# Weight conversion split between VectorE and GpSimd, or whole on VectorE; a second tile with a plain float32 second product

## The chip, the cores and the metric

The kernel runs on one core of a Trainium2 chip. The metric is the time of one execution on the device, in microseconds (us), lower is better. Three executions of the kernel before took 537.91 to 540.05 us, with a median of 540.05 us. One more was profiled; its time is 538.55 us, and the span from its first to its last instruction is 536.8 us.

Names used below: PE is TensorE (matrix products and transposes), DVE is VectorE, ACT is ScalarE, POOL is GpSimd, SP is the engine whose queue issues the DMAs. Each engine executes its own instructions in the order in which they were written; between engines there are semaphores.

## The reference

Windowed attention (8 batches, 8 heads, 576 positions, head size 64, each query sees itself and the 63 positions before it) is followed by a dense layer with a SoLU activation, a layer norm and a second product:

```python
scores = q @ k.T / sqrt(64);  masked outside 0 <= i - j < 64
attn = softmax(scores);  x = attn @ v            # x: 4608 tokens x 512
h = x @ w_in                                     # 4608 x 1024
solu = h * softmax(h)
ln = (solu - mean) / sqrt(var + 1e-6) * g_ln
out = ln @ w_out                                 # 4608 x 512, float32
```

**The two weights reach the kernel as 64-bit numbers** (`w_in` 512 x 1024, `w_out` 1024 x 512): the views that the kernel gets are double precision, read as pairs of 32-bit integers, and the kernel itself turns them into float32 by operations on the bits.

## The kernel before

**Tiles.** The 4608 tokens are 36 tiles of 128. For each tile t: scores (PE, into `pS`), masked row maxima (DVE, L396), exponentials (ACT, L401), division by the row sums (POOL, L419; on DVE for tile 0), transposes of the eight 128x128 blocks into `PT` (for tiles 0 to 4 by PE into the two-buffer PSUM tile `t` and copied out by ACT and DVE, L461; later by DMA), values (PE into `pX`, L480), the first product `pH` (PE), the SoLU and the norm (`moe_norm`: DVE L538 takes the row maximum, ACT L540 the exponential, DVE L543 the product with `pH`, ACT L549 the squares, a few small operations, POOL L556 a power and L560 the final scaling of `e`), transposes of `e`, the second product `pO` (PE), copy out and store.

**Products.** PE has a plain float32 product (L512 for the first product, L647 for the second) and a split one: both operands are divided into a high part in a reduced format and a low part that holds the rest, and three products are summed (high x high, high x low, low x high; L523 and L659). `PLAIN_IN = 3` tiles take the plain first product, `PLAIN_OUT = 1` tile the plain second one. The split needs the weights' high and low parts, which the function `split` makes once: for `w_in` four blocks of two halves, ACT L325 makes the high half and a subtraction (L327) the low half, on DVE for the half x = 0 and on POOL for x = 1; for `w_out` ACT L331 and DVE L333. Tiles with the plain second product multiply `g_ln` into `yH` on DVE while they copy it out of PSUM (L627); the others take a copy on ACT (L631) and a subtraction on DVE (L633).

**Weight conversion.** `weight_block` converts one of eight blocks of 128 x 2 x 512 numbers (0 to 3 of `w_in`, 4 to 7 of `w_out`), held in the ring `raw` of four buffers: the absolute value of the high word on ACT (L293), a clamp (L299), a mask and shift (L301), the sign joined in (L303), and the top bits of the low word joined in (L309). For `w_out` (`i >= HELPED`), the block is worked in two halves: ACT L296 shifts the low word, POOL does the clamp (L299) and adds the low word (L306), and DVE does L301 and L303.

**What sets the order.** A planner (`Plan`) is given every operation with its engine, an assumed cost and what it reads and writes, in program order. It lets PE and SP keep their program order (with the exception of some loose PE operations of the first tiles), gives every operation a due time that it derives from PE's, and simulates the engines; each engine then gets its operations in the simulated order. So a changed cost, key or call can move any operation on DVE, ACT and POOL. `RINGS` holds the number of buffers of each tile: `t` has 2, `pH`, `pS` and `pO` 1 each.

**Ahead and behind.** In step t of the main loop, scores and softmax are those of tile t + 3, transposes and values those of t + 1, and the second product is that of t - 2. `cross(t + 3)` (ACT copies and SP's DMA transposes that stand in for PE transposes from tile 5 on) is called last in the step. `split` of `w_out` stands ahead of the second product of tile `PLAIN_OUT`.

Of the kernel before, what the change touches and what calls it, by code (L numbers as in the profile page):

```python
# [37 lines left out]
PLAIN_OUT = 1  # L38
# [5 lines left out]
HELPED = 4  # L44
# [121 lines left out]
def tile_window_attention_solu_moe(  # L166
# [94 lines left out]
    def weight_block(i, src):  # L261

        def raw():
            return T("raw", i, [P, 2, 512, 2], I32)
# [4 lines left out]
        def tf():
            return W32(i)

        def lo():
# [4 lines left out]


        helped = i >= HELPED
        parts = (0, 1) if i == 0 or helped else (slice(0, 2),)
        if i:
            plan.dma(P * 8192, lambda: nc.sync.dma_start(
                raw().rearrange("p a n w -> p a (n w)"), src), [], [("raw", i, x) for x in parts])
        for x in parts:
            n = 1024 if x == slice(0, 2) else 512
            R, W = ("raw", i, x), ("w", i, x) if n == 512 else ("w", i)
            B = R + ("low",)
            if i == 0:  # L290
                plan.dma(P * 8 * n, lambda x=x: nc.sync.dma_start(
                    raw()[:, x].rearrange("p n w -> p (n w)"), src[:, x]), [], [R])
            plan.op("ACT", n + 66, lambda x=x: nc.scalar.activation(  # L293
                tf()[:, x], hi()[:, x].bitcast(F32), AF.Abs), [R], [W])
# [3 lines left out]
            plan.op("POOL" if helped else "DVE", n * 3 // 2 if helped else n // 3 * 2 + 18,
                    lambda x=x: (nc.gpsimd if helped else nc.vector).tensor_scalar(  # L299
                        tf()[:, x], tf()[:, x], EXP_HI, EXP_LO, ALU.min, ALU.max), [W], [W])  # L300
            plan.op("DVE", n // 3 * 2 + 18, lambda x=x: nc.vector.tensor_scalar(  # L301
                t()[:, x], t()[:, x], 0x07FFFFFF, 3, ALU.bitwise_and, ALU.logical_shift_left), [W], [W])
            plan.op("DVE", n + 170, lambda x=x: nc.vector.scalar_tensor_tensor(  # L303
                t()[:, x], hi()[:, x], -0x40000000, t()[:, x], ALU.bitwise_and, ALU.bitwise_or), [R, W], [W])
            if helped:
                plan.op("POOL", n * 2, lambda x=x: nc.gpsimd.tensor_tensor(  # L306
                    t()[:, x], t()[:, x], lo()[:, x], op=ALU.add), [B, W], [W])
            else:
                plan.op("DVE", n + 170, lambda x=x: nc.vector.scalar_tensor_tensor(  # L309
                    t()[:, x], lo()[:, x], 29, t()[:, x], ALU.logical_shift_right, ALU.bitwise_or), [R, W], [W])  # L310
# [8 lines left out]
    def split(i):  # L319

        for x in range(2):
            reads = [("w", i), ("w", i, x), ("w", NC + 1 if i < NC else NW - 1)]
            last = reads[:2] + [("H", i, x)], [("w", NW + i, x)]
            if i < NC:
                plan.op("ACT", 600, lambda x=x: nc.scalar.copy(WH(i, x), W32(i)[:, x]), reads, [("H", i, x)])  # L325
                plan.op("POOL" if x else "DVE", 1050 if x else 620, lambda x=x: (
                    nc.gpsimd if x else nc.vector).tensor_sub(  # L327
# [366 lines left out]
    for t in range(NTILE + BEHIND):  # L694
# [8 lines left out]
        if t < BEHIND:  # L703
# [72 lines left out]
```

## Time and profile before

| what | before |
|---|---|
| three runs, us | 540.05, 537.91, 540.05 |
| the profiled execution, us | 538.55 |
| its span, us | 536.8 |
| PE busy, us | 512.3 (95%) |
| DVE busy, us | 419.3 (78%) |
| ACT busy, us | 358.2 (67%) |
| POOL busy, us | 232.6 (43%) |
| mean granted TensorE clock | 0.993 |

Busy time is a sum over stages that differ. A window table of the same execution divides the span: PE is busy 7.26 of the 10 us from 50 to 60, 7.86 of those from 60 to 70, and all of those from 200 to 480. DVE is busy 10.00 us in each of the stretches 50 to 60 and 60 to 70, and 227.08 of the 280 us from 200 to 480. In rows of the timeline the columns are: start in us, duration in us, engine, line, operation, output and inputs with sizes, count; in brackets the idle time of the engine ahead of the row and what ended it. Rows of one engine may overlap by about 0.1 us, so the step from one start to the next, not the duration, is what an instruction costs its engine when it follows another.

### The profile page before, as it was taken

How to read it: one execution, taken by the hardware profiler on the slowest of the kernel's cores; microseconds unless marked ns; L12 is line 12 of the kernel's file. 1: busy time of each engine (PE TensorE's matmuls, PEld its weight loads, DVE VectorE, ACT ScalarE, POOL GpSimd, SP SyncE). 2: the span in 40 equal slices, each digit the busy share in tenths (PEclk: the TensorE clock that was granted, in tenths of full speed). 3: DMA queues.
4: the chain of work that ended last, by engine and by line, in shares of the span. 5: the costliest groups of instructions: out<-in, count | busy, mean ns of one | idle time of the engine just before them, and what ended most of it. 6: DMA issues, size and time to landing. Idle time of an engine off the chain costs nothing.

```text
span 536.8 us, 11697 instructions
## 1 busy us (share of the span) xinstructions
PE 512.3 (95%) x4080; PEld 396.9 (74%) x4080; DVE 419.3 (78%) x1323; ACT 358.2 (67%) x973; POOL 232.6 (43%) x426
## 2 busy tenths in 40 slices
PE   3779699999999999999999999999999999999997
PEld 2345468777878787877777777777777778787785
DVE  4959998788888788888887878888888888887630
ACT  5598667766766666666666766666666766666331
POOL 2149886244444444444444444444444444444220
PEclk9999799999999999999999999999999999999999
DMA  8992014879778878777788877777679877674411
GB/s 321 409 382 95 20 40 128 188 148 187 163 189 187 187 191 180 197 168 189 180 184 186 191 190 183 186 187 186 175 167 195 205 185 187 180 189 89 78 40 39
DMA packets 148506, 93.56 MB, mean 174 GB/s; under 512 B 132960, under 2 KB 132960, under 8 KB 148064
## 3 DMA queue, kind: packets, MB, share of 16 engines
q1 hardware_dynamic: 148448, 92.83, 68.4%
q8 instruction: 32, 0.52, 0.4%
q14 instruction: 26, 0.21, 0.1%
HBM read 50.86 MB, written 9.44 MB: 112 GB/s over the span
## 4 chain that ended last, share of the span: by engine, by line
PE 89%; DVE 5%; ACT 2%; DMA 2%; issue 1%; POOL 0%; POOLq 0%; DVEq 0%; ACTq 0%
PE pO L659 36%; PE pH L523 34%; PE pS L381 7%; PE pX L480 7%; PE pH L512 3%; PE pO L647 1%; PE pX L659 1%; DMA raw<-raw 1%; DVE w L301 1%; DVE sS L396 1%; DMA qk<-qk 1%; PE t L622 1%; DVE w L303 1%; DVE w L327 1%; ACT w L293 0%
## 5 line engine op out<-in xcount | busy, mean ns | idle before, releaser
L556 POOL TENSOR_TENSOR mst<-mst,neghalf 128x1 f32<-128x1 f32 x36 | 20.7, 574 | 238.7 <-DVE mst L554 238.7
L419 POOL TENSOR_SCALAR sS<-sS,rec 128x128 f32<-128x128 f32 x280 | 112.2, 419 | 20.2 <-DVE nmx L396 17.7
L401 ACT ACTIVATE sS<-sS,nmx 128x128 f32<-128x128 f32 x288 | 112.5, 396 | 7.5 <-DVE nmx L396 7.5
L659 PE MATMUL pO<-w_outH,yH 128*128 128x512 f32 x272 | 111.4, 410 | 0.0
L659 PE MATMUL pO<-w,yH 128*128 128x512 f32 x272 | 107.7, 396 | 0.0
L659 PE MATMUL pO<-w_outH,yL 128*128 128x512 f32 x272 | 107.0, 393 | 0.1
L523 PE MATMUL pH<-w_inH,xH 128*128 128x512 f32 x264 | 105.5, 399 | 0.0
L523 PE MATMUL pH<-w,xH 128*128 128x512 f32 x264 | 104.2, 399 | 0.0
L523 PE MATMUL pH<-w_inH,xL 128*128 128x512 f32 x264 | 103.6, 392 | 0.0
L494 ACT CAST xH<-pX 128x512 fp32r<-128x512 f32 x33 | 19.3, 586 | 115.7 <-PE pX L480 115.7
L560 POOL TENSOR_SCALAR e<-e,mst 128x512 f32<-128x512 f32 x72 | 72.5, 1014 | 17.1 <-DVE rec L414 9.5
L433 ACT COPY raw<-sS 128x1024 uint16<-128x1024 uint16 x62 | 62.2, 1049 | 4.7 <-POOL sS L419 4.7
L538 DVE TENSOR_REDUCE mst<-pH 128x1 f32<-128x1024 f32 x36 | 44.0, 1223 | 25.1 <-PE pH L523 24.1
L659 PEld LDWEIGHTS pO<-w_outH,yH 128*128 128x128 f32 x272 | 51.0, 187 | 16.5 <-issue 5.2
L586 DVE COPY raw<-e 128x1024 uint16<-128x1024 uint16 x62 | 45.5, 735 | 21.6 <-POOL e L560 21.6
L659 PEld LDWEIGHTS pO<-w_outH,yL 128*128 128x128 f32 x272 | 51.1, 188 | 13.1 <-DVE yL L633 0.5
L523 PEld LDWEIGHTS pH<-w_inH,xH 128*128 128x128 f32 x264 | 49.5, 187 | 13.3 <-ACT sS L401 0.2
L523 PEld LDWEIGHTS pH<-w_inH,xL 128*128 128x128 f32 x264 | 49.6, 188 | 12.6 <-issue 0.2
L659 PEld LDWEIGHTS pO<-w,yH 128*128 128x128 f32 x272 | 51.1, 188 | 10.5
L523 PEld LDWEIGHTS pH<-w,xH 128*128 128x128 f32 x264 | 49.6, 188 | 11.4
L401 ACT ACTIVATION_READ_ACCUMULATOR sS<-sS,nmx 128x1 f32 x288 | 55.3, 192 | 0.0
L396 DVE CUSTOM_DVE_ANT_0 sS<-pS,maskNone 128x128 f32<-128x128 f32 x224 | 51.4, 282 | 1.4 <-PE pS L381 1.3
(77 smaller groups left out, 804.3 us busy)
## 6 DMA issues: line engine op xcount, KB each, us to landing
qk<-qk SPq DMA_DIRECT2D x36, 640.0 KB, 4.6
v<-vS SPq DMA_DIRECT2D x36, 512.0 KB, 5.2
y<-ot SPq DMA_DIRECT2D x36, 256.0 KB, 2.5
raw<-w_out SPq DMA_DIRECT2D x4, 1024.0 KB, 9.5
raw<-w_in SPq DMA_DIRECT2D x3, 1024.0 KB, 11.8
raw<-raw SPq DMA_TRANSPOSE x124, 3.2
raw<-w_in SPq DMA_DIRECT2D x2, 512.0 KB, 6.6
g_sb<-gT SPq DMA_DIRECT2D x1, 4.0 KB, 14.2
```

Of the source, the lines that this page charges most:

```text
L381: nc.tensor.matmul(PS(t)[half * WIN:(half + 1) * WIN, r, p], q[rs, p, half * WIN:(half + 1) * WIN], keys, start=True, stop=True)
L396: plan.op("DVE", 215, lambda h=h: nc.vector.tensor_tensor_reduce(SS(t)[:, h], PS(t)[:, h % 2, h // 2], mk, scale=-SCALE, scalar=BIG, op0=A ...
L401: plan.op("ACT", 390, lambda h=h: nc.scalar.activation(SS(t)[:, h], SS(t)[:, h], AF.Exp, bias=cols("nmx", h), scale=-1.0, accum_out=cols(" ...
L419: plan.op(engine, cost, lambda h=h: v.tensor_scalar(SS(t)[:, h], SS(t)[:, h], rec()[:, h:h + 1], 0.0, ALU.mult, ALU.add), [R], [("sS", t, h)])
L433: plan.op("ACT", 1050, lambda x=x: nc.scalar.copy(XP(t)[:, x], SS(t)[:, 4 * x:4 * x + 4].bitcast(U16).rearrange("p h (n w) -> p w (h n)", ...
L480: nc.tensor.matmul(PX(t)[r * D:(r + 1) * D, p, ks], V(t, half)[:, h * D:(h + 1) * D], PT(t)[:, h, ks], start=True, stop=True)
L523: plan.op("PE", 233, lambda n=n, c=c, x=x, w=w: nc.tensor.matmul(PH(t)[:, hs], x(t)[:, c], WH(c, h) if w is WH else WL(c)[:, h], start=(n ...
L538: plan.op("DVE", 1150, lambda: nc.vector.tensor_reduce(nmax(), PH(t), axis=AX.X, op=ALU.max, negate=True), [("pH", t)], [key(0)])
L556: plan.op("POOL", 560, lambda: nc.gpsimd.tensor_tensor(kk(), kk(), neghalf, op=ALU.pow), [], [key(5)])
L560: plan.op("POOL", 770, lambda h=h, hs=hs: nc.gpsimd.tensor_scalar(E(t)[:, hs], E(t)[:, hs], nmean(), kk(), ALU.add, ALU.mult), [key(4), ke ...
L586: plan.op("DVE", 740, lambda h=h: nc.vector.tensor_copy(EP(t, h), E(t)[:, h * 512:(h + 1) * 512].bitcast(U16).rearrange("p (n w) -> p w n" ...
L659: plan.op("PE", 233, lambda f=f, i=i, x=x, k=k, y=y, w=w: nc.tensor.matmul(PO(), y(t)[:, f], w(i, x), start=(f == k == 0), stop=(f == NF - ...
```

## The change

- `weight_block` has one form again: all eight blocks are converted on DVE (clamp, mask and shift, sign, low word), blocks 1 to 7 whole (1024 elements a partition), block 0 in its two halves. ACT's shift of the low word (L296) and POOL's clamp (L299) and addition (L306) are gone.
- The low parts of `w_in` (L327 before, L310 after) are all made on DVE.
- `PLAIN_OUT` is 2: tile 1 too takes the plain second product, and `split` of `w_out` moves one step later with it.
- `cross` is called right behind the softmax of its tile, ahead of the second product of that step, where it was called at the end of the step.

```diff
-PLAIN_OUT = 1
+PLAIN_OUT = 2
-HELPED = 4
...
-        helped = i >= HELPED
-        parts = (0, 1) if i == 0 or helped else (slice(0, 2),)
-        if i:
-            plan.dma(P * 8192, lambda: nc.sync.dma_start(
-                raw().rearrange("p a n w -> p a (n w)"), src), [], [("raw", i, x) for x in parts])
+        parts = (0, 1) if i == 0 else (slice(0, 2),)
         for x in parts:
...
             plan.op("ACT", n + 66, lambda x=x: nc.scalar.activation(
                 tf()[:, x], hi()[:, x].bitcast(F32), AF.Abs), [R], [W])
-            if helped:
-                plan.op("ACT", n + 66, lambda x=x: nc.scalar.mul(
-                    lo()[:, x], lo()[:, x].bitcast(U32), 2.0 ** -29), [R], [B])
-            plan.op("POOL" if helped else "DVE", n * 3 // 2 if helped else n // 3 * 2 + 18,
-                    lambda x=x: (nc.gpsimd if helped else nc.vector).tensor_scalar(
-                        tf()[:, x], tf()[:, x], EXP_HI, EXP_LO, ALU.min, ALU.max), [W], [W])
+            plan.op("DVE", n // 3 * 2 + 18, lambda x=x: nc.vector.tensor_scalar(
+                tf()[:, x], tf()[:, x], EXP_LO, EXP_HI, ALU.max, ALU.min), [W], [W])
...
-            if helped:
-                plan.op("POOL", n * 2, lambda x=x: nc.gpsimd.tensor_tensor(
-                    t()[:, x], t()[:, x], lo()[:, x], op=ALU.add), [B, W], [W])
-            else:
-                plan.op("DVE", n + 170, lambda x=x: nc.vector.scalar_tensor_tensor(
-                    t()[:, x], lo()[:, x], 29, t()[:, x], ALU.logical_shift_right, ALU.bitwise_or), [R, W], [W])
+            plan.op("DVE", n + 170, lambda x=x: nc.vector.scalar_tensor_tensor(
+                t()[:, x], lo()[:, x], 29, t()[:, x], ALU.logical_shift_right, ALU.bitwise_or), [R, W], [W])
...
-                plan.op("POOL" if x else "DVE", 1050 if x else 620, lambda x=x: (
-                    nc.gpsimd if x else nc.vector).tensor_sub(
+                plan.op("DVE", 620, lambda x=x: nc.vector.tensor_sub(
                     WL(i)[:, x], W32(i)[:, x], WH(i, x).bitcast(F32)), *last)
...
+    def attend(t):
+        on(scores, t + AHEAD)
+        on(softmax, t + AHEAD)
+        on(cross, t + AHEAD)
...
-            on(scores, t + AHEAD)
-            on(softmax, t + AHEAD)
+            attend(t)
...
-        on(cross, t + AHEAD)
```

In the changed kernel the lines stand 8 to 17 earlier: L299 is L287, L301 L289, L303 L291, L309 L293, L327 L310, L396 L379, L419 L402, L461 L444, L538 L521, L543 L526, L627 L610, L622 L605, L647 L630, L523 L506.

What the planner makes of it is shown at three places. In the names, the first number is that of the tile or block (`w_5` is weight block 5, `w_8` to `w_11` are the low parts of blocks 0 to 3, `PT_3` belongs to token tile 3), the second one is only an identifier.

The first place is DVE ahead of the copy of `PT_3`, the second half of tile 3's transposed weights. Before:

```order
L303 SCALAR_TENSOR_TENSOR w_5_443<-raw_5_310,w_5_443 128x512
L301 TENSOR_SCALAR w_5_443<-w_5_443 128x512
L327 TENSOR_TENSOR w_8_206<-w_0_151,w_inH_103 128x512
L303 SCALAR_TENSOR_TENSOR w_5_443<-raw_5_310,w_5_443 128x512
L301 TENSOR_SCALAR w_6_549<-w_6_549 128x512
L327 TENSOR_TENSOR w_9_596<-w_1_192,w_inH_103 128x512
L303 SCALAR_TENSOR_TENSOR w_6_549<-raw_6_377,w_6_549 128x512
L301 TENSOR_SCALAR w_6_549<-w_6_549 128x512
...
L303 SCALAR_TENSOR_TENSOR w_6_549<-raw_6_377,w_6_549 128x512
...
L301 TENSOR_SCALAR w_7_584<-w_7_584 128x512
L461 COPY PT_3_564<-t_13_616 128x512
```

and after:

```order
L291 SCALAR_TENSOR_TENSOR w_5_432<-raw_5_304,w_5_432 128x1024
L289 TENSOR_SCALAR w_6_448<-w_6_448 128x1024
L293 SCALAR_TENSOR_TENSOR w_5_432<-raw_5_304,w_5_432 128x1024
L291 SCALAR_TENSOR_TENSOR w_6_448<-raw_6_367,w_6_448 128x1024
L287 TENSOR_SCALAR w_7_468<-w_7_468 128x1024
L293 SCALAR_TENSOR_TENSOR w_6_448<-raw_6_367,w_6_448 128x1024
L289 TENSOR_SCALAR w_7_468<-w_7_468 128x1024
L444 COPY PT_3_559<-t_13_588 128x512
```

The rows ahead of the first one are, in both kernels, the eight row maxima of tile 4 with L543 of tile 1 among them. The two subtractions for the low parts of `w_in` no longer stand ahead of the copy, and the conversions are whole blocks.

The second place is the rest of that stretch on DVE, behind the copy, after the change:

```order
L521 TENSOR_REDUCE mst_2_604<-pH_2_557 128x1
L610 TENSOR_TENSOR yH_0_628<-t_2_598,g_sb_105 128x512
L291 SCALAR_TENSOR_TENSOR w_7_468<-raw_7_412,w_7_468 128x1024
L610 TENSOR_TENSOR yH_0_628<-t_3_606,g_sb_105 128x512
L293 SCALAR_TENSOR_TENSOR w_7_468<-raw_7_412,w_7_468 128x1024
L526 ISA e_2_630,mst_2_604<-pH_2_557,e_2_630 128x1024
...
L478 TENSOR_TENSOR xL_3_664<-pX_3_611,xH_3_652 128x512
L310 TENSOR_TENSOR w_8_668<-w_0_151,w_inH_103 128x512 x2
L397 TENSOR_SCALAR rec_4_674<-sm_4_541 128x8
L310 TENSOR_TENSOR w_9_678<-w_1_193,w_inH_103 128x512 x2
L400 RECIPROCAL rec_4_674<-rec_4_674 128x8
L310 TENSOR_TENSOR w_10_685<-w_2_208,w_inH_103 128x512 x2
```

Behind these stand the last two L310 (`w_11`). All eight low parts of `w_in` are now made in one run here, where four of them stood on POOL and two of DVE's four stood ahead of the copy.

The third place is POOL, whose rows between the scaling of tile 3's and tile 4's attention weights were, before:

```order
L419 TENSOR_SCALAR sS_3_407<-sS_3_407,rec_3_496 128x128 x8
L299 TENSOR_SCALAR w_5_443<-w_5_443 128x512
L306 TENSOR_TENSOR w_4_436<-w_4_436,raw_4_275 128x512
L299 TENSOR_SCALAR w_6_549<-w_6_549 128x512
L306 TENSOR_TENSOR w_5_443<-w_5_443,raw_5_310 128x512
...
L306 TENSOR_TENSOR w_7_584<-w_7_584,raw_7_419 128x512
L327 TENSOR_TENSOR w_11_715<-w_3_268,w_inH_103 128x512
L419 TENSOR_SCALAR sS_4_534<-sS_4_534,rec_4_695 128x128 x8
```

and are, after, with the rows around them:

```order
L539 TENSOR_TENSOR mst_0_334<-mst_0_334,neghalf_106 128x1
L543 TENSOR_SCALAR e_0_356<-e_0_356,mst_0_334 128x512 x2
L402 TENSOR_SCALAR sS_3_401<-sS_3_401,rec_3_495 128x128 x8
L402 TENSOR_SCALAR sS_4_518<-sS_4_518,rec_4_674 128x128 x8
L539 TENSOR_TENSOR mst_1_477<-mst_1_477,neghalf_106 128x1
```

Nothing is left between the two L402. PE's rows behind tile 1's second product, 1651 up to the last instruction, read alike in both kernels; the 24 split products of tile 1's second product (L659) are eight plain ones (L630). In the profile a plain product of 512 columns shows as two instructions, so that eight of them count 16.

More of the change, by code (lines that the diff above doesn't have):

```diff
@@ L14 @@
 I32 = mybir.dt.int32
-U32 = mybir.dt.uint32
 AF = mybir.ActivationFunctionType
@@ L278, in hi @@
             return raw()[:, :, :, 1]
-        helped = i >= HELPED
-        parts = (0, 1) if i == 0 or helped else (slice(0, 2),)
-        if i:
-            plan.dma(P * 8192, lambda: nc.sync.dma_start(
-                raw().rearrange("p a n w -> p a (n w)"), src), [], [("raw", i, x) for x in parts])
-        for x in parts:
[L287 to L292, printed above, removed]
+        parts = (0, 1) if i == 0 else (slice(0, 2),)
+        for x in parts:
+            n = 1024 if i else 512
+            R, W = ("raw", i, x), ("w", i) if i else ("w", i, x)
+            plan.dma(P * 8 * n, lambda x=x: nc.sync.dma_start(
+                raw()[:, x].rearrange("p a n w -> p a (n w)" if i else "p n w -> p (n w)"), src[:, x]), [], [R])
             plan.op("ACT", n + 66, lambda x=x: nc.scalar.activation(
                 tf()[:, x], hi()[:, x].bitcast(F32), AF.Abs), [R], [W])
-            if helped:
-                plan.op("ACT", n + 66, lambda x=x: nc.scalar.mul(
-                    lo()[:, x], lo()[:, x].bitcast(U32), 2.0 ** -29), [R], [B])
-            plan.op("POOL" if helped else "DVE", n * 3 // 2 if helped else n // 3 * 2 + 18,
-                    lambda x=x: (nc.gpsimd if helped else nc.vector).tensor_scalar(
-                        tf()[:, x], tf()[:, x], EXP_HI, EXP_LO, ALU.min, ALU.max), [W], [W])
+            plan.op("DVE", n // 3 * 2 + 18, lambda x=x: nc.vector.tensor_scalar(
+                tf()[:, x], tf()[:, x], EXP_LO, EXP_HI, ALU.max, ALU.min), [W], [W])
             plan.op("DVE", n // 3 * 2 + 18, lambda x=x: nc.vector.tensor_scalar(
@@ L718, in tile_window_attention_solu_moe @@
             on(values, t + 1)
-            on(scores, t + AHEAD)
-            on(softmax, t + AHEAD)
+            attend(t)
             if t - BEHIND == PLAIN_OUT:
```

## Prediction

> **What bounds the kernel now.** I read the page's chain of waits first, then windows of PE with the granted clock, then the timelines of PE, DVE and POOL where PE stands still.
>
> ```profile
> span 536.8 us, 11697 instructions
> ...
> PE 89%; DVE 5%; ACT 2%; DMA 2%; issue 1%; POOL 0%; POOLq 0%; DVEq 0%; ACTq 0%
> ...
> 50.00:62.00 12.00, 7.26 (x23) 0.97 0.16 64
> 62.00:68.00 6.00, 5.86 (x69) 0.50 0.25 87
> 68.00:74.00 6.00, 6.00 (x15) 0.98 0.01 1
> ...
> 200.00:480.00 280.00, 280.00 (x2335) 223.53 (x2334) 227.08 (x738) 193.89 (x534) 121.70 (x231) 1.00 0.77 185
> ```
>
> The window columns are stretch, length, PE busy with its count, and, in the first three rows, clock, DMA share and GB/s. The chain is PE for 89%, and PE is busy all of 200 to 480 us, so the steady part is PE's own work. What can be won lies ahead of it: from 50 to 62 PE works 7.26 of 12 us, and then 6 us pass at half clock. The order of events on PE:
>
> ```profile
> 49.28 6.25 PE L512 MATMUL pH<-w,xH 128*128 128x512 f32 x14 [0.34 <-DVE mst L543]
> 55.36 0.60 PE L456 MATMUL t<-ident,sS 128*128 128x128 f32 x4
> ...
> 56.66 0.60 PE L622 MATMUL t<-ident,e 128*128 128x128 f32 x4
> 62.14 1.12 PE L622 MATMUL t<-ident,e 128*128 128x128 f32 x4 [4.88 <-DVE PT L461]
> 63.19 1.98 PE L480 MATMUL pX<-PT,v 128*64 128x64 f32 x32
> 65.10 1.99 PE L381 MATMUL pS<-qk 64*64 64x128 f32 x32
> 67.02 7.70 PE L647 MATMUL pO<-w,yH 128*128 128x512 f32 x16
> 74.15 0.79 PE L523 MATMUL pH<-w_inH,xH 128*128 128x512 f32 x1
> ...
> 81.01 1.03 PE L622 MATMUL t<-ident,e 128*128 128x128 f32 x8
> 81.97 1.15 PE L480 MATMUL pX<-PT,v 128*64 128x64 f32 x32
> 83.05 1.10 PE L381 MATMUL pS<-qk 64*64 64x128 f32 x32
> 84.09 0.50 PE L659 MATMUL pO<-w_outH,yH 128*128 128x512 f32 x1
> ...
> 89.80 0.40 PE L523 MATMUL pH<-w_inH,xH 128*128 128x512 f32 x1
> ```
>
> PE stands 4.88 us until DVE's copy of `PT` (L461) frees a buffer of `t`. The same three groups at 62.14 and at 81.01 show what the low clock costs on top: from start to start 1.05 against 0.48 us for four transposes (half of the 0.96 for eight), 1.91 against 1.08, 1.92 against 1.04.
>
> Why is the copy late?
>
> ```profile
> 45.20 0.77 DVE L414 TENSOR_SCALAR rec<-sm 128x8 f32<-128x8 f32 x1
> ...
> 50.99 1.52 DVE L301 TENSOR_SCALAR w<-w 128x512 int32<-128x512 int32 x1
> 52.44 1.09 DVE L327 TENSOR_TENSOR w<-w,w_inH 128x512 fp32r<-128x512 f32 x1
> 53.45 1.79 DVE L303 SCALAR_TENSOR_TENSOR w<-raw,w 128x512 int32<-128x512 int32 x1
> ...
> 61.41 0.68 DVE L461 COPY PT<-t 128x512 f32<-128x512 f32 x1
> ...
> L303 DVE SCALAR_TENSOR_TENSOR w<-raw,w 128x512 int32<-128x512 int32 x8 | 9.0, 1126 | 0.0
> L538 DVE TENSOR_REDUCE mst<-pH 128x1 f32<-128x1024 f32 x2 | 2.4, 1218 | 0.4 <-PE pH L512 0.4
> L543 DVE CUSTOM_DVE_ANT_0 e<-pH,e 128x1024 f32<-128x1024 f32 x2 | 2.4, 1214 | 0.0
> ...
> 50.49 1.73 POOL L306 TENSOR_TENSOR w<-w,raw 128x512 int32<-128x512 int32 x1
> 52.96 1.73 POOL L306 TENSOR_TENSOR w<-w,raw 128x512 int32<-128x512 int32 x1
> ```
>
> DVE is not idle, but its instructions last far longer than the work in them. L301 starts at 50.99 and ends at 52.51, just behind POOL's L306 (50.49 to 52.22); L303 of 53.45 lasts 1.79, and POOL's next L306 ends at 54.69. The same operations with POOL idle, twice as wide:
>
> ```profile
> 24.73 0.69 DVE L299 TENSOR_SCALAR w<-w 128x1024 f32<-128x1024 f32 x1 [0.41 <-ACT w L293]
> 25.34 0.28 DVE L396 CUSTOM_DVE_ANT_0 sS<-pS,maskNone 128x128 f32<-128x128 f32 x1
> ...
> 25.55 0.69 DVE L301 TENSOR_SCALAR w<-w 128x1024 int32<-128x1024 int32 x1
> ...
> 26.36 1.22 DVE L303 SCALAR_TENSOR_TENSOR w<-raw,w 128x1024 int32<-128x1024 int32 x1
> ...
> 28.31 1.22 DVE L309 SCALAR_TENSOR_TENSOR w<-raw,w 128x1024 int32<-128x1024 int32 x1
> 29.45 0.17 DVE L414 TENSOR_SCALAR rec<-sm 128x8 f32<-128x8 f32 x1
> ```
>
> A whole block costs 1.22 us where a half takes 1.126 us in the mean beside POOL. From start to start, the clean costs are 0.61 (L299, and L301 alike), 0.21 (L396) and 1.14 us (L309, and L303 alike).
>
> The Trainium skill, SBUF — State Buffer, section "SBUF: two separate sides", says that the two engines share a port pair that one instruction holds to its end while the other engine blocks. By that rule the stall above is POOL's doing, and the rows agree; it also speaks against part of the change, below.
>
> **The change part by part.**
>
> *DVE up to the copy.*
>
> ```profile
> 40.66 0.57 DVE L557 TENSOR_TENSOR mst<-mst 128x1 f32<-128x1 f32 x1 [2.79 <-POOL mst L556]
> ```
>
> Up to L414 at 45.20 I move nothing: the first `w_out` block, 2 x 0.61 + 2 x 1.14 = 3.5 us, goes mostly into this idle time of 2.79, and what it pushes back is ahead of L538 of tile 1, which waits for PE. From 45.20 to the copy DVE then has L414, L417 and one L301 (0.9 together), eight L396 (8 x 0.21 = 1.7), L543 (1.15), four block operations of two tensors (4 x 1.14 = 4.6) and three of one (3 x 0.61 = 1.8): 10.2 us, so the copy starts at 55.4 and ends at 56.0, where it was 61.41. POOL has in this stretch only the eight L419 of tile 3; DVE's L396, L414 and L543 stand beside them.
>
> *PE at the stall.* L543 of tile 1, for which PE waited at 49.28, ends some 0.8 us earlier, since DVE's first rows from 45.20 lose the waits for POOL. So all of PE moves by 0.8: the first L622 starts at 55.85 and the second can at 56.3, when the copy is there. PE goes on at 56.3 instead of 62.14: 5.8 us. Nothing is left that would bring the clock down, so the half-clock excess goes too: 0.57 + 0.83 + 0.88, and for L647, 7.13 from start to start against 16 x 0.434 = 6.95 at full clock ((55.36 - 49.28)/14 = 0.434), 0.18 more: 2.5 us. The first product of tile 3, at 74.15 before, would start at 74.15 - 8.3 = 65.8.
>
> *The plain second product.* 16 x 0.434 = 6.95 us replace 24 split products, 89.80 - 84.09 = 5.71: 1.24 us more on PE, uncovered. On DVE L627 takes the place of L633, alike in kind. The low parts of `w_out` are due 14 us later.
>
> *The low parts of `w_in`.* All eight now stand behind L543 of tile 2 and in front of PE's first split product. Behind the copy DVE has L538 (it waits for PE until 56.0), L627 twice, two block operations, L543, L495: I count 56.1 + 1.15 + 2 x 0.6 + 2 x 1.14 + 1.15 + 0.6 = 62.5, then eight L327 at 0.6 and about 0.5 of small ones: the seventh ends at 67.2, the last at 67.8. PE wants the seventh after eight high products and three low ones (11 x 0.238, from 5.71/24): 65.8 + 2.6 = 68.4. But POOL's eight L419 for tile 4 start in the middle of them:
>
> ```profile
> 69.54 0.67 DVE L327 TENSOR_TENSOR w<-w,w_inH 128x512 fp32r<-128x512 f32 x1
> ...
> 37.30 2.80 POOL L419 TENSOR_SCALAR sS<-sS,rec 128x128 f32<-128x128 f32 x8 [4.39 <-DVE nmx L396]
> 72.11 3.67 POOL L419 TENSOR_SCALAR sS<-sS,rec 128x128 f32<-128x128 f32 x8
> ...
> 77.34 3.04 POOL L560 TENSOR_SCALAR e<-e,mst 128x512 f32<-128x512 f32 x2 [0.51 <-DVE mst L557]
> ```
>
> Alone an L419 takes 2.80/8 = 0.35, at 72.11, with DVE at work, 0.46. At best nothing is lost; at worst each of the four or five L327 left waits for one L419, 0.35 each, 1.8 us, and the seventh is 0.6 late. The norm of tile 1 (L552, L556, L560) stands behind this and is wanted at 65.8 + 24 x 0.238 + 0.96 of transposes = 72.5; its two L560 took 3.04 us beside DVE, and I count them ready between 72.3 and 73.9, up to 1.4 late. So 0 to 2.0 us of new idle time; I take 0.7, since most of the excess is measured at 0.11 an L419.
>
> By the skill's rule of the held port, L327 with its two SBUF inputs and L419 exclude each other in full; that is the 2.0 end.
>
> *No cost.* ACT loses eight L296, POOL its clamps, additions and subtractions, neither of which ended the stall. Calling `cross` earlier puts SP's transposes ahead of a store that nothing on the chip waits for; the loads stay behind both. What hides it is PE's work: were SP to hold a load, PE would stop in each of some 30 steps.
>
> *Sum* against the profiled execution, 538.55: -8.3 + 1.24 + 0.7 = -6.4, so 532.2. It lies 1.5 below the median of the three runs, which reach from 537.91 to 540.05; midway between 532.2 and 540.05 - 6.4 = 533.7 I forecast **533.0 us**.
>
> **The rivals.**
>
> 1. *The queue of low parts becomes the wait.* All eight L327 wait for an L419 each (2.8 us): the seventh is 1.3 late, and the norm of tile 1, 2.8 behind and slowed, 2.2 more: idle of 3.5 instead of 0.7, 535.0 on the profile, about 535.8. For it: DVE's longest run of two-input operations now lies right ahead of the first split product. Against: POOL begins only after the fourth L327.
>
> The Trainium skill, TensorE: Matmul & The Clock Gate, section "What's actually happening", has the clock halved after an idle window of about 3.4 us; by it, this rival's 3.5 us in one piece would cost the 2.5 of the low clock as well, 538.3. The 4.88 us above agree with it.
>
> 2. *Slower: DVE's times were no contention.* If the 1.126 of a half block is its price in this stage, work given back to a full engine makes it later. DVE's rows of 45.20 to 61.41 are 9.7 us at the clean costs and took 16.2, a factor of 1.68; with it the copy starts at 45.2 + 17.1 = 62.3, 0.9 later than before; the run from there to the seventh L327, 11.8 us clean, takes 19.8 and ends at 82.1; PE, at low clock, wants it at 63.4 + 4.9 + 7.1 + 2.6 = 78.0, a wait of 4; the plain product adds 1.24: +6, 543 to 546. The case decides where DVE needs over 16.2 us from L414 to the copy. Against it: 1.22 for a whole block with POOL idle.
>
> 3. *Given back later.* The front is 6.4 us earlier, but SP's new order (transposes, then store) makes PE wait in the steady part, by 0.2 us in each of 30 tiles: 538 to 540, no change. Against: PE had no idle time in 280 us, and its order there is the same.
>
> **How the numbers follow.** Forecast 0.64, rival 1 0.20, rival 2 0.07, rival 3 0.09. A measurement of this kernel can tell about 0.5% (2.7 us) from no change, so faster means under 537.3: the forecast and most of rival 1, 0.81; same: rival 3 and the edge of rival 1, 0.12; slower 0.07. The range: no new idle and the lower runs give 531, with 1.5 us for the spread of runs 529.5; above, it takes in rival 1 and the beginning of rival 3: 538.0. All the range but its last 0.7 us lies on the side of faster.
>
> **What would show it.** DVE's `PT` copy at about 55.4, without an idle row of over 1 us in PE ahead of the second L622; clock 1.00 from 56 to 68; L630 as 16 in about 6.95 us from about 59; `pH` of tile 3 at 66, and of tile 4 at 83 to 84 (89.80 before). L291 at 1.22 whole would settle rival 2. Idle time on PE with L310 or L543 as releaser at 67 to 75 would be rival 1; PE idle behind 100 us rival 3. I am wrong if the copy is not before 58 or a gap of over 3 us opens elsewhere.

## Result and the profile after

| | before | after |
|---|---|---|
| runs, us | 537.91 to 540.05, median 539.86 (4 runs) | 530.94 to 533.39, median **531.04** (4 runs) |
| ratio, 95% interval | 1 | **0.9855** [0.982, 0.9891] |
| profiled execution, span, us | 536.8 | 531.6 |
| PE busy; DVE; ACT; POOL, us | 512.3; 419.3; 358.2; 232.6 | 511.5; 415.4; 352.4; 213.9 |

The changed kernel is faster by 1.1 to 1.8%. The forecast was 533.0 us with a range of 529.5 to 538.0. Three executions that took far longer than the others of their kernel (873.66 us of the kernel before, 2703.8 and 572.57 us in two of the experiments) are left out of all medians and ranges here and below. The page of the changed kernel, and its window table of PE (stretch, length, busy time and count of PE, PEld, DVE, ACT, POOL, then clock, DMA share and GB/s):

```profile
span 531.6 us, 11607 instructions
...
PE 94%; ACT 2%; DVE 2%; DMA 1%; POOL 0%; issue 0%; ACTq 0%; DVEq 0%
...
20.00:30.00 10.00, 7.76 (x60) 3.77 (x60) 7.71 (x27) 4.98 (x20) 0.00 (x0) 0.83 1.02 405
50.00:62.00 12.00, 12.00 (x98) 6.95 (x97) 12.00 (x19) 10.27 (x28) 0.68 (x2) 1.00 0.39 139
62.00:68.00 6.00, 6.00 (x16) 2.80 (x16) 6.00 (x15) 3.79 (x7) 1.19 (x2) 1.00 0.02 10
```

PE now works 12.00 of the 12 us from 50 to 62 (7.26 before), and the stretch from 62 to 68 is at clock 1.00 (0.50 before). DVE's share of the chain fell from 5% to 2%. But a stretch from 20 to 30 us is at 0.83, which no stretch of before was at that time. PE's timeline of this execution shows a group of four products that lasts 3.41 us, where the same group took 1.98 before:

```profile
24.91 3.41 PE L495 MATMUL pH<-w,xH 128*128 128x512 f32 x4 [1.00 <-ACT xH L473]
```

The first transfer also landed 0.6 us later in this execution (PE's first product at 5.17 us, 4.54 before). A second profiled execution of the same changed kernel, with a span of 529.3 us and its first product at 4.56, has no such group, so its rows can be laid beside those of before. PE:

```profile
47.74 6.18 PE L495 MATMUL pH<-w,xH 128*128 128x512 f32 x14
...
55.06 1.04 PE L605 MATMUL t<-ident,e 128*128 128x128 f32 x8
56.02 1.15 PE L463 MATMUL pX<-PT,v 128*64 128x64 f32 x32
57.10 1.10 PE L364 MATMUL pS<-qk 64*64 64x128 f32 x32
58.14 7.13 PE L630 MATMUL pO<-w,yH 128*128 128x512 f32 x16
64.71 0.80 PE L506 MATMUL pH<-w_inH,xH 128*128 128x512 f32 x1
...
67.90 1.51 PE L439 MATMUL t<-ident,sS 128*128 128x128 f32 x8
...
72.95 0.65 PE L605 MATMUL t<-ident,e 128*128 128x128 f32 x4 [0.32 <-POOL e L543]
...
75.65 7.13 PE L630 MATMUL pO<-w,yH 128*128 128x512 f32 x16
82.22 0.80 PE L506 MATMUL pH<-w_inH,xH 128*128 128x512 f32 x1
82.86 0.40 PE L506 MATMUL pH<-w,xH 128*128 128x512 f32 x1
```

The wait of 4.88 us is gone: all eight L605 run in one piece. DVE ahead of it:

```profile
44.51 0.16 DVE L397 TENSOR_SCALAR rec<-sm 128x8 f32<-128x8 f32 x1
...
51.10 1.21 DVE L291 SCALAR_TENSOR_TENSOR w<-raw,w 128x1024 int32<-128x1024 int32 x1
52.24 0.68 DVE L287 TENSOR_SCALAR w<-w 128x1024 f32<-128x1024 f32 x1
52.84 1.21 DVE L293 SCALAR_TENSOR_TENSOR w<-raw,w 128x1024 int32<-128x1024 int32 x1
53.97 0.68 DVE L289 TENSOR_SCALAR w<-w 128x1024 int32<-128x1024 int32 x1
54.58 0.68 DVE L444 COPY PT<-t 128x512 f32<-128x512 f32 x1
```

The whole block costs 1.21, and the copy starts at 54.58 (61.41 before), 10.07 us behind L397; 10.2 were forecast.

### The profile page after: what moved, and what is told of

It is laid out like the page before. It is cut to its first block, busy times and chain, and to the rows that moved or that the text cites. A ratio compares the mean times of both kernels' runs of the same rounds, so it can differ in the third digit from the quotient of the medians.

```text
span 531.6 us, 11607 instructions
## 1 busy us (share of the span) xinstructions
PE 511.5 (96%) x4072; PEld 393.2 (74%) x4072; DVE 415.4 (78%) x1327; ACT 352.4 (66%) x959; POOL 213.9 (40%) x406
## 4 chain that ended last, share of the span: by engine, by line
PE 94%; ACT 2%; DVE 2%; DMA 1%; POOL 0%; issue 0%; ACTq 0%; DVEq 0%
PE pO L642 36%; PE pH L506 34%; PE pX L463 7%; PE pS L364 7%; PE pH L495 4%; PE pO L630 3%; PE pX L642 1%; DMA qk<-qk 1%; PE t L605 1%; ACT sS L384 1%; PE t L439 1%; ACT w L285 0%; POOL e L543 0%; DVE mst L521 0%; ACT e L523 0%; ACT PT L444 0%
## 5 line engine op out<-in xcount | busy, mean ns | idle before, releaser
L402 POOL TENSOR_SCALAR sS<-sS,rec 128x128 f32<-128x128 f32 x280 | 116.9, 439 | 49.8 <-DVE nmx L379 27.0
L642 PE MATMUL pO<-w_outH,yH 128*128 128x512 f32 x264 | 108.1, 410 | 0.0
L506 PE MATMUL pH<-w_inH,xH 128*128 128x512 f32 x264 | 105.8, 401 | 0.0
L642 PE MATMUL pO<-w,yH 128*128 128x512 f32 x264 | 104.6, 396 | 0.0
L506 PE MATMUL pH<-w,xH 128*128 128x512 f32 x264 | 104.2, 399 | 0.0
L642 PE MATMUL pO<-w_outH,yL 128*128 128x512 f32 x264 | 103.7, 393 | 0.0
L506 PE MATMUL pH<-w_inH,xL 128*128 128x512 f32 x264 | 103.6, 392 | 0.0
L543 POOL TENSOR_SCALAR e<-e,mst 128x512 f32<-128x512 f32 x72 | 73.5, 1028 | 18.4 <-DVE rec L397 11.0
L521 DVE TENSOR_REDUCE mst<-pH 128x1 f32<-128x1024 f32 x36 | 44.0, 1224 | 26.0 <-PE pH L506 25.2
L569 DVE COPY raw<-e 128x1024 uint16<-128x1024 uint16 x62 | 46.6, 752 | 21.9 <-POOL e L543 21.9
L642 PEld LDWEIGHTS pO<-w_outH,yH 128*128 128x128 f32 x264 | 49.5, 187 | 16.0 <-issue 5.0
L506 PEld LDWEIGHTS pH<-w_inH,xH 128*128 128x128 f32 x264 | 49.5, 188 | 13.5 <-issue 0.5
L506 PEld LDWEIGHTS pH<-w_inH,xL 128*128 128x128 f32 x264 | 49.6, 188 | 12.6 <-DVE w L310 0.2
L642 PEld LDWEIGHTS pO<-w_outH,yL 128*128 128x128 f32 x264 | 49.6, 188 | 12.3
L506 PEld LDWEIGHTS pH<-w,xH 128*128 128x128 f32 x264 | 49.6, 188 | 11.6 <-issue 0.2
L642 PEld LDWEIGHTS pO<-w,yH 128*128 128x128 f32 x264 | 49.6, 188 | 10.2
L379 DVE CUSTOM_DVE_ANT_0 sS<-pS,maskNone 128x128 f32<-128x128 f32 x224 | 51.1, 281 | 4.0 <-PE pS L364 3.9
```

The lines of the kernel that those rows point to most:

```text
L379: plan.op("DVE", 215, lambda h=h: nc.vector.tensor_tensor_reduce(SS(t)[:, h], PS(t)[:, h % 2, h // 2], mk, scale=-SCALE, scalar=BIG, op0=A ...
L402: plan.op(engine, cost, lambda h=h: v.tensor_scalar(SS(t)[:, h], SS(t)[:, h], rec()[:, h:h + 1], 0.0, ALU.mult, ALU.add), [R], [("sS", t, h)])
L506: plan.op("PE", 233, lambda n=n, c=c, x=x, w=w: nc.tensor.matmul(PH(t)[:, hs], x(t)[:, c], WH(c, h) if w is WH else WL(c)[:, h], start=(n ...
L521: plan.op("DVE", 1150, lambda: nc.vector.tensor_reduce(nmax(), PH(t), axis=AX.X, op=ALU.max, negate=True), [("pH", t)], [key(0)])
L543: plan.op("POOL", 770, lambda h=h, hs=hs: nc.gpsimd.tensor_scalar(E(t)[:, hs], E(t)[:, hs], nmean(), kk(), ALU.add, ALU.mult), [key(4), ke ...
L569: plan.op("DVE", 740, lambda h=h: nc.vector.tensor_copy(EP(t, h), E(t)[:, h * 512:(h + 1) * 512].bitcast(U16).rearrange("p (n w) -> p w n" ...
```

## Experiments

The kernel before ran beside each of them, with medians of 538.6 to 538.9 us; a ratio is the time of a run over that of the kernel before, with its 95% interval. Line numbers of a run can stand a few higher than in the kernel it was made from. "Added" instructions work on a spare tile whose contents nothing reads, or on a PSUM buffer that is overwritten later, so that they change no result.

### The parts of the change alone

The conversion alone, in the kernel before:

```diff
-HELPED = 4
+HELPED = 8
```

> The kernel before, with the conversion of w_out whole on DVE (no GpSimd, no ScalarE part in it) and nothing else changed: the low parts of w_in stay divided between DVE and GpSimd, one tile has the plain second product. My theory (the stall before the second L622, and the low clock behind it, come from GpSimd's conversions holding up DVE): the PT copy of tile 3 comes some 5 us earlier, PE does not stand still there, clock 1.00 from 56 to 68, and the time falls by 6.5 to 8.5 us against the kernel before. Rival (the moved low parts of w_in are what freed DVE ahead of the copy): less than half of the gain, 536 to 538. Rival (the plain second product of tile 1 is needed for the gain, since w_out's low parts have to be made in 70 to 80 us): the stall moves to the second product of tile 1, 535 to 538.

Measured: 534.02 us (533.51 to 535.18), ratio 0.9906 [0.9893, 0.9919]. The conversion alone brings two thirds of the gain, less than was expected. PE's timeline tells why:

```profile
57.98 0.66 PE L622 MATMUL t<-ident,e 128*128 128x128 f32 x4 [0.73 <-DVE PT L461]
...
75.99 0.66 PE L622 MATMUL t<-ident,e 128*128 128x128 f32 x4 [0.87 <-POOL e L560]
...
92.23 1.28 PE L480 MATMUL pX<-PT,v 128*64 128x64 f32 x32 [1.15 <-issue]
94.34 1.10 PE L381 MATMUL pS<-qk 64*64 64x128 f32 x32 [0.83 <-DMA qk<-qk]
```

The wait for the copy is 0.73 instead of 4.88, but PE, earlier now, runs into the next waits: POOL's scaling of `e`, and at 92 to 94 tile 5's transposed weights and loads. Even the 0.73 has the old cause: one POOL subtraction (L327, 53.07 to 55.03 us) is left ahead of the copy, and DVE's L299 beside it, at 53.83, takes 1.76 us, where the changed kernel's takes 0.68.

The plain second product alone, in the kernel before:

```diff
-PLAIN_OUT = 1
+PLAIN_OUT = 2
```

> The kernel before, with the plain second product for tile 1 too and nothing else changed. My theory: PE gets 1.24 us more work and the stall at 57 to 62 us stays: 1 to 1.5 us slower than before. Rival (the plain product takes work from DVE and ScalarE at a crowded place and gains by itself): 0.5 to 2 us faster.

Measured: 539.75 us (538.26 to 541.17, 11 runs), ratio 1.0018 [1.0007, 1.0028], 0.4 to 1.5 us slower. PE's wait is 4.88 as before, and 62 to 68 us are at clock 0.50. So alone it costs about what was put down for it, and the rival's gain did not come.

The whole change without the plain second product of tile 1:

```diff
-PLAIN_OUT = 2
+PLAIN_OUT = 1
```

> The changed kernel with the plain second product for tile 0 alone, as before the change. My theory (the second plain product costs PE 1.24 us and buys nothing): 1.0 to 1.3 us faster than the changed kernel, about 529.8. Rival (the eight low parts of w_out, 5.3 us of DVE, then fall due right behind those of w_in, and PE waits for them): as slow as the changed kernel or slower, 531 to 533, with PE idle on L316 at 78 to 83 us.

Measured: 536.71 us (534.66 to 538.82, 12 runs), ratio 0.9958 [0.9944, 0.9973]. It is 5.5 us slower than the changed kernel where 1.0 to 1.3 faster was expected. **The theory of an edit that only costs fell here.** PE has no idle time at the old stall in this run either, nor does it wait for L316 at 78 to 83 us as the rival had it. It loses the time later:

```profile
90.30 1.09 PE L463 MATMUL pX<-PT,v 128*64 128x64 f32 x16 [2.13 <-issue]
92.07 1.12 PE L463 MATMUL pX<-PT,v 128*64 128x64 f32 x16 [0.67 <-DVE PT L426]
93.67 1.99 PE L364 MATMUL pS<-qk 64*64 64x128 f32 x32 [0.48 <-DMA qk<-qk]
```

DVE's and SP's timelines of the same run say what is late:

```profile
78.97 1.40 DVE L316 SCALAR_TENSOR_TENSOR w<-w,g_sb,w_outH 128x512 fp32r<-128x512 f32 x2
80.30 0.15 DVE L397 TENSOR_SCALAR rec<-sm 128x8 f32<-128x8 f32 x1
...
84.42 3.31 SPq L419 DMA_TRANSPOSE raw<-raw  x2
```

and the same rows of the changed kernel (the execution with a span of 529.3):

```profile
74.67 0.16 DVE L397 TENSOR_SCALAR rec<-sm 128x8 f32<-128x8 f32 x1
...
78.48 0.75 DVE L316 SCALAR_TENSOR_TENSOR w<-w,g_sb,w_outH 128x512 fp32r<-128x512 f32 x1
...
77.78 2.71 SPq L419 DMA_TRANSPOSE raw<-raw  x2
```

With one plain product the low parts of `w_out` (L316) are due for tile 1 already, and all eight stand ahead of tile 5's row sums (L397); with two, only two of the eight do. The row sums come 5.6 us later, POOL's scaling, ACT's copies and SP's transposes follow, and PE, which wants tile 5's weights at 88.1, waits.

To tell whether it is that place on DVE or the split product itself, the changed kernel was given six more instructions of the kind of L316 in the same place, with the plain products kept:

```diff
+            def sums(s=s):
+                for _ in range(6 if t == 5 else 0):
+                    nc.vector.scalar_tensor_tensor(
+                        spare[:, 0], spare[:, 0], g_sb[:, :1], spare[:, 1], ALU.mult, ALU.subtract)
+                nc.vector.tensor_scalar_add(rec()[:, s], T("sm", t, [P, H], pool=st)[:, s], 1e-9)
```

> The changed kernel with six more VectorE instructions of the kind of L316 (128x512, scalar_tensor_tensor, on a spare tile that nothing else reads) directly ahead of tile 5's row-sum step L397; every engine's order is otherwise the same and the second products are all as in the changed kernel. Theory (in the kernel with one plain second product the 5.5 us went to VectorE's queue: eight L316 instead of two ahead of tile 5's L397): six by 0.66 us shift L397 of tile 5 by 4.0 us, POOL's scaling, ACT's copies and SP's transposes follow, the last copy L426 of tile 5 ends at 88 to 89.5 and the norm of tile 3 comes as late; PE waits 2 to 5.5 us ahead of L605 or L463 at 88 to 90: 533.5 to 537. Rival (the split product itself lost the time there, not the place of its low parts): not more than 0.8 slower than the changed kernel, 531 to 533.5.

Measured: 536.05 us (535.75 to 536.29), ratio 0.9952 [0.9938, 0.9967]: 4.8 slower than the changed kernel, so work at that place on DVE is enough to lose the time, with the plain products kept. But PE does not stop at L605 or L463, as was expected, but 3 us behind them:

```profile
74.71 4.67 DVE L401 SCALAR_TENSOR_TENSOR spare<-spare,g_sb 128x512 f32<-128x512 f32 x6
79.30 0.17 DVE L403 TENSOR_SCALAR rec<-sm 128x8 f32<-128x8 f32 x1
...
92.56 0.69 DVE L576 COPY raw<-e 128x1024 uint16<-128x1024 uint16 x1 [0.51 <-POOL e L550]
...
94.30 1.28 DVE L623 TENSOR_TENSOR yL<-t,yH 128x512 fp32r<-128x512 f32 x2
...
95.03 0.80 PE L649 MATMUL pO<-w_outH,yL 128*128 128x512 f32 x1 [2.86 <-DVE yL L623]
95.63 0.63 PE L649 MATMUL pO<-w_outH,yH 128*128 128x512 f32 x1
96.06 0.63 PE L649 MATMUL pO<-w,yH 128*128 128x512 f32 x1
```

Tile 5's weights are just in time; the norm of tile 3, whose product with `pH` on DVE is 4.6 us late too, is not. DVE stands waiting for `e` of tile 3, and behind that in its order is the low part of tile 2's second product (L623), for which PE waits 2.86 us. The split products behind it start 0.43 us apart instead of 0.235, at half clock. So two chains leave DVE at 75 us with little to spare, and which of them stops PE depends on what stands there.

### What POOL does to DVE

Half of `w_in`'s low parts back on POOL, in the changed kernel:

```diff
-                plan.op("DVE", 620, lambda x=x: nc.vector.tensor_sub(
+                plan.op("POOL" if x else "DVE", 1050 if x else 620, lambda x=x: (
+                    nc.gpsimd if x else nc.vector).tensor_sub(
```

> The changed kernel with the second halves of the low parts of w_in on GpSimd again. My theory: PE does not wait for low parts in the changed kernel, so their move brings nothing by itself; four GpSimd operations of some 1.4 us come ahead of the scaling of tile 4's attention weights and hold up DVE meanwhile: 0 to 2 us slower than the changed kernel, 531 to 533. Rival (the move of the low parts is part of the gain): 3 us slower or more.

Measured: 534.06 us (532.71 to 535.85, 6 runs), ratio 0.9909 [0.9891, 0.9926], some 3 us slower than the changed kernel's median: 0 to 2 had been expected, and the rival's 3 came. PE waits 0.73 us for the copy and 0.88 for `e`, as in the conversion alone. These waits put tile 1's second product 1.5 us later than in the changed kernel (77.16 against 75.65); the rest of the difference was not followed. So beside two plain second products, the low parts in one run on DVE are the better of the two.

The cause of the old stall was tested by bringing it back. Eight additions of two 128x512 tiles on POOL, at the time of the conversions, no other engine's order changed:

```diff
+    for _ in range(8):
+        plan.op("POOL", 1450, lambda: nc.gpsimd.tensor_tensor(
+            spare[:, 0], spare[:, 0], spare[:, 1], op=ALU.add), [("rec", 3, 0)], [("spare",)])
```

> The changed kernel with eight additional additions of two 128 x 512 float32 tiles on GpSimd, behind its scaling of tile 3's attention weights, on a spare tile that nothing else uses (the result is not part of the output). Every other engine has the same instructions in the same order as the changed kernel. My theory (a DVE instruction that reads two SBUF operands, or runs at two elements a cycle, waits until GpSimd's two-input instruction has ended): DVE's block operations from 50 us on last up to 1.3 us longer each, the copy of PT for tile 3 comes 4 to 7 us later, PE stands still before the second L605 for 3 to 6 us and runs at half clock behind it; 4 to 9 us slower than the changed kernel, 535 to 540. Rival (what slowed DVE before were the half blocks and their number, not GpSimd): DVE's times and the time of the kernel stay as they are, 531 to 533.

Measured: 539.85 us (538.38 to 541.71, 9 runs), ratio 1.0018 [1.0001, 1.0035]; the whole gain is gone. POOL, DVE and PE of this run:

```profile
50.03 15.23 POOL L717 TENSOR_TENSOR spare<-spare 128x512 f32<-128x512 f32 x8
...
52.74 2.29 DVE L295 SCALAR_TENSOR_TENSOR w<-raw,w 128x1024 int32<-128x1024 int32 x1
...
57.18 1.75 DVE L289 TENSOR_SCALAR w<-w 128x1024 f32<-128x1024 f32 x1
...
63.45 1.12 PE L607 MATMUL t<-ident,e 128*128 128x128 f32 x4 [6.10 <-DVE PT L446]
```

Each block instruction of DVE is 1.07 to 1.08 us longer (2.29 against 1.21, 1.75 against 0.68), and PE waits 6.10 us. The Trainium skill, SBUF — State Buffer, section "SBUF: two separate sides", has one engine blocked until the other's instruction ends; these rows agree.

Is it POOL's being busy, or the data it moves? Twenty powers of 128x1 in the same place:

```diff
+    for _ in range(20):
+        plan.op("POOL", 560, lambda: nc.gpsimd.tensor_tensor(
+            spare, spare, neghalf, op=ALU.pow), [("rec", 3, 0)], [("spare",)])
```

> The changed kernel with twenty additional powers of one column (128 x 1) on GpSimd at the same place, about 11 us of GpSimd time as well, on a spare column that nothing else uses. All other engines have the same order. If it is the time for which GpSimd's instruction holds what the two engines share, then these hold it too, for about 0.56 us each: DVE's operations wait up to 0.5 us each and the kernel is 1 to 5 us slower than the changed one. If it is the data that GpSimd moves, then no wait shows: 531 to 533.

Measured: 531.2 us (530.08 to 532.58), ratio 0.986 [0.9837, 0.9882], no difference from the changed kernel:

```profile
50.04 18.36 POOL L717 TENSOR_TENSOR spare<-spare,neghalf 128x1 f32<-128x1 f32 x20
...
51.67 1.21 DVE L295 SCALAR_TENSOR_TENSOR w<-raw,w 128x1024 int32<-128x1024 int32 x1
```

The twenty stretch over 18.36 us, longer than the eight additions, and DVE does not notice. So POOL's being at work is not enough. The powers differ from the additions in width (1 column against 512) and in operation, and no run parts these two; that it is the amount of data is argued, not shown.

The changed kernel once more beside these:

> The changed kernel once more, on the chip of these runs, as the reference for the other three. 530.5 to 533.5. In its profile above, PE ran at half clock for some us at 25 to 29 us, which made 1.6 us; without that the span is 529 to 530.

Measured: 531.26 us (531.08 to 532.86, 5 runs), ratio 0.9871 [0.9851, 0.989].

### The half clock

In the kernel before, five plain products were added on PE between the two L622, where it waits:

```diff
+            if t == 0 and h == 0:
+                for _ in range(5):
+                    plan.op("PE", 0, lambda: nc.tensor.matmul(
+                        T("pO", 0, [P, DM], pool=ps_o), ident, spare, start=True, stop=True),
+                        [], [("pO", 0)])
```

> The kernel before with five plain 128 x 512 products on PE between the two L622 of tile 0, into the PSUM bank of the second product before it is first used (the result is overwritten, not part of the output). All other engines keep their order. The five take 4.3 us at full clock of the 4.88 us for which PE stands still. My theory (the half clock at 62 to 68 us is due to PE's idle time and costs 2.5 us): clock 1.00 from 57 to 68, and 2.0 to 2.5 us faster than before. Rival (the low clock has another cause, or the time behind it is set by DVE's low parts of w_in): clock unchanged, or the same time as before within 0.5 us.

Measured: 537.96 us (537.21 to 538.97, 11 runs), ratio 0.9984 [0.9972, 0.9997]: 0.8 us faster in the mean, not 2.0 to 2.5. The windows of this run against the clock of 0.50 that stood there before:

```profile
62.00:68.00 6.00, 5.35 (x75) 3.33 (x74) 6.00 (x10) 2.19 (x4) 5.23 (x5) 1.00 0.26 85
```

The low clock comes from the wait, since it goes when the wait is filled. The 2.5 us are there too: from the second part of tile 2's first product to the first product of tile 3 PE needs 22.27 us (50.73 to 73.00) where it needed 24.87. But of these 2.6 us, 1.8 are given back up to tile 1's second product (11.72 us against 9.94), with waits for POOL and DVE of 0.21, 0.23 and 0.73 us at 77 to 82 us: in the kernel before, what PE wants next is only just ready.

Two more kernels added such products to the changed kernel in the first 30 us, where PE's clock is low and the group of 3.41 us was seen:

```diff
+    fill(2, [])
     load(0, range(1))
     prep(0)
     scores(0)
+    fill(3, [("pS", 0, 1)])
...
+    fill(1, [("pX", 0, 1)])
     scores(1)
+    fill(1, [("pS", 1, 1)])
...
             scores(2)
+            fill(1, [("pS", 2, 1)])
```

> The changed kernel with eight more plain products on PE whose results nothing reads: two ahead of tile 0's scores, three behind them, one each behind tile 0's values, tile 1's scores and tile 2's scores. Theory (PE's early low clock and the half-clock spell near 25 us cost time and come from PE's idle time): the first scores take 1.1 instead of 1.98 us, no spell in any execution, 529.5 to 531.0 with a spread under 1 us. Rival (the first 30 us are bound by the loads and VectorE's conversions, and the spell has another cause): 531 to 533.5 in the same two groups, or up to 1 us slower from the added products.

> As the kernel with eight added products, but with only the three in the gaps of PE at 16 to 28 us. Theory (the spell near 25 us comes from the gaps there): no execution with the spell, 530.5 to 531.8, all within 0.8 us. Rival (the spell has another cause): two groups, 531.0 to 531.5 and 532.6 to 533.6, as in the changed kernel.

Measured: all eight, 530.7 us (530.28 to 532.61, 4 runs), ratio 0.986 [0.9838, 0.9882]; the last three alone, 531.58 (531.01 to 532.87, 4 runs), ratio 0.9873 [0.9855, 0.9891]. Neither can be told from the changed kernel. With all eight the first scores take 1.44 us instead of 1.98 (1.1 was expected); each kernel still has one execution of four that is over a microsecond longer than the rest. The slow stretch did not go away. PE with three added products, and last the same group in the kernel of the next section, which has none:

```profile
34.31 0.69 PE L465 MATMUL pX<-PT,v 128*64 128x64 f32 x16 [0.96 <-ACT PT L446]
34.93 1.06 PE L366 MATMUL pS<-qk 64*64 64x128 f32 x16
35.92 5.81 PE L497 MATMUL pH<-w,xH 128*128 128x512 f32 x10
...
36.49 5.43 PE L495 MATMUL pH<-w,xH 128*128 128x512 f32 x10
```

Ten products took 4.56 us before the change, 5.81 with the added products and 5.43 without them. So a stretch at 35 us needs no added product. And it needs no long gap: with the three products no gap of PE in the 20 us ahead is over 0.96 us. What starts it is not settled; the last section has what the traces say.

### The moved call

`cross` at the end of the step again, in the changed kernel:

```diff
-        on(cross, t + AHEAD)
...
             on(moe_out, t - BEHIND, *([t - BEHIND + 1] if last else []))
+        on(cross, t + AHEAD)
```

> The changed kernel with cross called at the end of the step again, as before the change. Theory (the prediction's 'no cost'): no difference, 530.5 to 533.5, PE without idle time from 200 to 480 us. Rival (the earlier SP transposes are what made tile 5's weights come in time): PE waits over 0.5 us at 88 to 92 us and the time is 532.5 to 536.

Measured: 532.85 us (531.13 to 533.05, 4 runs), ratio 0.9883 [0.986, 0.9905], which overlaps the changed kernel's own. PE is busy 280.00 of the 280 us from 200 to 480, and the runs fall at 531.1 and 532.8 to 533.1, where the changed kernel's fall as well. No effect is shown, as the "no cost" said.

## Why the prediction was right, and which of its steps were not

Beside the changed kernel's execution with a span of 529.3 us, the steps read so. In brackets is the start of a row before and now, DVE's in the first step and PE's in the others; each step counts only what it adds to the steps above it, and the last line is their sum:

| step | forecast, us | measured, us |
|---|---|---|
| up to L414 (45.20, now 44.51) | 0 | -0.69 |
| arrival at the second part of tile 2's first product (49.28, now 47.74), behind that | -0.8 | -0.85 |
| the wait, and the half clock behind it, up to the first product of tile 3 (74.15, now 64.71) | -7.5 | -7.90 |
| new waits up to tile 1's second product (84.09, now 75.65) | +0.7 | +1.00 |
| eight plain products instead of 24 (90.03 less 84.09, now 82.86 less 75.65) | +1.24 | +1.27 |
| sum | -6.4 | -7.2 |

The 90.03 is the second split product of tile 4 before the change, taken in both kernels because the first one behind plain products shows 0.4 longer. The spans differ by 7.5; the 0.3 that are left fall behind this stage and were not followed. The medians differ by 8.8 in the result and by 7.6 in the larger set of runs (538.82 and 531.26). The forecast sum was 0.8 too small: a gain of 0.7 was put at nothing and the half clock at 0.4 too little, against 0.3 too little for new waits.

**The stall.** The mechanism was right in each part: DVE's times were contention with POOL (shown by the eight additions that bring it back, and by 1.21 for whole blocks), rival 2 is out, and the copy came 10.07 us behind L397 where 10.2 were forecast. The half clock was undersized by 0.4: L647's 7.13 from start to start was set against 16 x 0.434 = 6.95, but in the changed kernel, at full clock, the next row starts 6.57 behind L630 (64.71 less 58.14).

**"Up to L414 at 45.20 I move nothing"** failed by 0.69. The change reaches DVE earlier too. Before, one of tile 0's scalings lasted 1.29 us, where the changed kernel has 0.28:

```profile
15.11 1.72 POOL L327 TENSOR_TENSOR w<-w,w_inH 128x512 fp32r<-128x512 f32 x1 [10.48 <-ACT w_inH L325]
...
15.62 1.29 DVE L419 TENSOR_SCALAR sS<-sS,rec 128x128 f32<-128x128 f32 x1
```

```profile
15.52 0.28 DVE L402 TENSOR_SCALAR sS<-sS,rec 128x128 f32<-128x128 f32 x1
```

PE is 0.6 us ahead from there on. The long row stands beside POOL's first subtraction for the low parts of `w_in` (15.11 to 16.83 us), which the changed kernel does not have: the same contention as at the stall, in a place where the prediction did not look for it. In the conversion alone that subtraction comes at 53.07 us instead, and the scaling takes 0.28 there too.

**The low parts** of `w_in` cost what rival 1 feared in kind but not in size. The eight L310 and the eight L402 of tile 4 meet:

```profile
64.53 4.50 POOL L402 TENSOR_SCALAR sS<-sS,rec 128x128 f32<-128x128 f32 x8 [16.16 <-DVE rec L400]
```

It is POOL that waits, not DVE as the prediction's worst case had it: the eight L402 take 4.50 us instead of 2.80, while the L310 stay at 0.60 to 0.71 from start to start. PE's eight L439, which need the scaled weights, take 1.51 instead of 1.04, and L605 waits 0.32. Rival 1's 3.5 us did not come.

**The plain second product** was the step that failed, though its number was right. It was priced as 1.24 us of pure cost, and the price is confirmed twice (+1.27 in the rows, 0.4 to 1.5 alone). What was left out is what it releases: the prediction noted that the low parts of `w_out` "are due 14 us later" and gave that no value. In the changed kernel it is worth about 5.5 us net, because PE is 7 us earlier than before and DVE's queue at 71 to 80 us would then be the bound. In the kernel before, PE's later wish for tile 5's weights left room, so there the plain product only cost. The parts do not add up:

| median, us | tile 1 split | tile 1 plain |
|---|---|---|
| low parts of `w_in` shared with POOL, blocks whole on DVE | 534.02 | 534.06 |
| low parts of `w_in` all on DVE | 536.71 | 531.04 |

(The upper left kernel calls `cross` late, which shows no effect by itself.) All low parts on DVE are worse than shared ones with one plain product, and better with two. The sum of the prediction came out since it priced the whole change at once. That no further wait opens behind tile 1's second product was not worked out in it, and that it came so was luck. Of the parts, it priced the second plain tile at +1.24 us, where it is worth about -5.5 in the changed kernel, and the low parts on DVE at +0.7, where they are worth about -3.0 there: it would have been wrong about these two by some 7 and 4 us.

**Rival 3** is out: PE has no idle time from 200 to 480 us with either place of `cross`.

## What to carry to other kernels

Where a stall on the leading engine is removed, walk on from the new, earlier times to the next things it will want, and look for work on the engine that feeds it that could be due later; an edit that costs the leading engine a microsecond can be what keeps the gain. Look for VectorE rows that are too long for their size beside GpSimd rows of large tiles: the time is in the pairing, not in either. Parts of a change that move work on a shared queue should be tried together as well as alone.

## What was not expected of the hardware

- **Slow stretches of PE with no long gap ahead of them.** In some executions of one kernel, PE runs a stretch at half clock between 12 and 39 us, and the time is about 1.6 us longer: five runs of the changed kernel gave 531.08, 531.24, 531.26 and 532.84, 532.86, with a mean clock of 0.999 to 1.0 in the first three and 0.996 in the others. The granted clock in the traces has a grain: in the changed kernel's execution with a span of 531.6 us it is 0.50 for 3.41 us (25.33 to 28.74), behind the wait of 4.88 us before the change it was 0.50 for 6.83 us (61.37 to 68.19), and in each execution all its changes lie whole multiples of 3.41 us apart. In the 3.41 us ahead of 25.33, PE was busy for 1.75 us, in pieces with no gap over 1.00 us; in the execution with a span of 529.3 us, which has no stretch, the emptiest 3.41 us of the grain from 16 us on have 1.86 us. The grain starts at another time in each execution, so the same rows can fall on it differently. That this decides whether a stretch comes is suggested, not shown, and no limit can be read off: ahead of the stretches at 35 us PE was busy for 2.40 of the 3.41 us.
- **A wait of 2 to 3 us was followed by half clock.** With six added instructions on DVE, PE waits 2.86 us, and the clock is 0.50 from 94.93 to 98.34 us; in the changed kernel with one plain second product it waits 2.13 us, and the clock is 0.50 from 90.37 to 97.20. The Trainium skill, TensorE: Matmul & The Clock Gate, section "What's actually happening", speaks of an idle window of about 3.4 us. The grain of 3.41 us agrees with that, but in the 3.41 us ahead of these two stretches PE was busy for 0.67 and 1.28 us: here the measurement decides, and the window need not be idle throughout.
- **Small GpSimd instructions leave VectorE alone.** Twenty of them on 128x1 cost DVE nothing, while eight on 128x512 cost it 1.07 us for each of its block instructions. It is POOL that waits: one of the powers takes 0.55 us at 58.35 us and another 1.42 us at 51.86, where DVE works on whole blocks. The Trainium skill, SBUF — State Buffer, section "SBUF: two separate sides", has no exception for small ones; by the rows there is one, since the block instruction that DVE starts at 58.70 us, while the power from 58.35 to 58.90 still runs, takes its usual 1.22 us.
